# One PSUM bank set aside for the first upper products of each expert's first chunk

## The chip, the cores and the metric

The kernel runs on one core of one Trainium2 chip. The metric is the device time of one execution in microseconds (us). Three runs of the kernel before gave 606.06, 604.7 and 606.04 us, median 606.04.

## What is computed

The reference chains three parts. First comes attention (2 batches, 8 heads, 768 positions, head size 64; each position sees 4 sink positions and a window of 128). Its output, 1536 tokens of 512 numbers, goes through a dense pair of products (512 to 2048 to 512, with a leaky step between). Last comes a layer of 8 experts, and the change lies there:

```
logits = x @ w_gate;  expert_idx = argmax(logits)
# each token takes the next free row of its expert, up to capacity = 384
h = max(einsum('ecd,edf->ecf', disp, w1), 0)     # 512 -> 1024, "upper"
y = einsum('ecf,efd->ecd', h, w2)                # 1024 -> 512, "lower"
out[i] = gate_w[i] * y[expert_idx[i], pos[i]]
```

With the reference's inputs the router sends 715, 147, 16, 240, 4, 20, 277 and 117 tokens to experts 0 to 7.

## The kernel before, in words

An expert's rows are cut into chunks of 128: a capacity of 384 gives up to three chunks per expert, written (e, 0), (e, 1), (e, 2). The number of rows of an expert is known only while the kernel runs. So chunk (e, 0) is always computed, and chunks (e, 1) and (e, 2) stand in conditional parts, one inside the other (`further_chunks`, `guard`, branches on line L1327). Chunk (0, 0) is computed earlier in most cases; the experts' stage only repeats it under a condition on `more` (L1366 and L1367). With these inputs the `more` part is skipped, (0, 1), (0, 2), (1, 1), (3, 1), (6, 1) and (6, 2) are computed, and the conditional parts of experts 2, 4, 5 and 7 are skipped whole.

One chunk is computed in four steps. `turn_in` (L431 to L433) turns the rows with four TensorE transposes and splits them into a high and a low half (ACT, then DVE). `expert_up` (L1262, L1267) makes two products of 512 columns, 12 matmuls each (three per slice of 128, for the two halves of both factors); ACT evicts each from PSUM through a Relu into `hh`. `turn_hidden` (L1282 to L1286) turns the hidden rows, ACT (`hth`) and DVE (`htl`) split them. `expert_down` (L1298) adds up 24 matmuls, a scaled eviction `yo` follows (L1305, or L1303 in the last chunk), and POOL scatters the rows to the output (L1308). The weights arrive by DMA in pieces (L1214 on the SP queue) and are split by ACT (L1196) and DVE (L1197).

The stage has all eight PSUM banks. They are named es0 to es2, et0 to et3 and eo0, and the list `every` has them in that order. Three rings share them: "t" (es0 to es2) for what is turned, "u" (et0, et1, et2) for upper products, "y" (et3, eo0) for lower products. `next_bank` goes round a ring at build time, whether a conditional part will run or not:

```python
banks = {"t": every[:3], "u": every[3:6], "y": every[6:]}
```

In this ring an expert's three chunks take six upper banks, so (e, 0) always gets et0 and et1, (e, 1) et2 and et0, (e, 2) et1 and et2. Expert 0 is the exception in the text of the program: `more` holds (0, 0) with et0 and et1, and (0, 1) follows with et2 and et0.

The order on each engine is the order of the program's text. What one engine waits for on another is a count of that other's finished instructions. A skipped conditional part is left through an instruction of its own on each engine (an event semaphore on the branch's line): it waits until the engine's own earlier work is done and then adds to the count all that the skipped part would have added. So a matmul that writes a bank last read by ACT in a skipped conditional part waits until ACT itself has come past that part.

Around the end of the dense part stand these steps, in TensorE's order: `first_y` (L489, lower product of chunk (0, 0), in bank eo0, evicted by ACT at L496), the skipped `more` part (L1366, L1367), `turn_in_slot(1, 0)` (L431, into the bank that `next_bank("y")` gives), and `further_chunks(0, 1)` (L1249, L1327, L1262). From expert 1 on, the loop does `expert_up(e, 0)`, two turns in, `expert_down(e - 1, 0)`, `turn_hidden(e, 0)` and then the conditional part of e; the next thing on TensorE after that part is `expert_up(e + 1, 0)`.

Of the kernel before, what the change touches and what calls it, by code (L numbers as in the profile page):

```python
# [35 lines left out]
def attention_mlp_moe_kernel(  # L36
# [84 lines left out]
    def slot(tag, dt=F32R):  # L121
        slot_n[tag] = slot_n.get(tag, 0) + 1
        return slot_pool[tag].tile([P, SW], dt, tag=tag, name=f"{tag}_{slot_n[tag]}", bufs=1)
# [7 lines left out]
    for bl in range(NT // XB):  # L131
        for kp in range(KD // 2):
            for hl in range(2):
                t = slot(f"x{(bl * (KD // 2) + kp) * 2 + hl}")
# [182 lines left out]
    def bank(tag, name, shape=(P, 512)):  # L317

        if not shared:
            tag = tag[-1].replace("x", "t")  # L320
            return psum[0].tile(list(shape), F32, tag=tag, name=name, bufs=n_bank[tag])
        banks_ = bank_sets[tag[:-1]][tag[-1]]
        n = bank_at[tag] = bank_at.get(tag, -1) + 1
        return psum[0].tile(
            list(shape), F32, tag=f"b{banks_[n % len(banks_)]}", name=name, bufs=1
        )
# [295 lines left out]
    with ExitStack() as actx:  # L622
# [12 lines left out]
        for n in range(QA):  # L635
            t = ap_c.tile([P, 2, S], F32, name=f"qa{n}")
# [36 lines left out]
        if small:  # L673
            for n in range(3):
                t = ap_c.tile([P, 2, 4, D1], F32, name=f"vsk{n}")
                nc.gpsimd.memset(t, 0.0)
                vsks.append(t)
                t = ap_c.tile([P, P], F32, name=f"pk{n}")
# [190 lines left out]
        for b in range(B):  # L869
            for hp in range(H // 2):  # L870
# [3 lines left out]
                for i0 in range(0, NQ, 2):  # L874
                    t = Item()
                    t.st, t.n, t.nm, t.units = st, len(groups), f"{st.nm}_{i0}", []
                    for ii in range(min(2, NQ - i0)):
                        u = Item()
# [32 lines left out]
        def at(xs, n):  # L911
            return xs[n] if 0 <= n < len(xs) else None
# [23 lines left out]
        for n in range(nu + 11):  # L936
            u = at(units, n)
# [292 lines left out]

    ep.append(ctx.enter_context(tc.tile_pool(name="ep", bufs=2, side="right")))
    every = [bank(tag, f"e{tag}{n}") for tag in "sto" for n in range(n_bank[tag])]
    banks = {"t": every[:3], "u": every[3:6], "y": every[6:]}
    bank_n = {}

    def next_bank(nm):
        n = bank_n[nm] = bank_n.get(nm, -1) + 1
        return banks[nm][n % len(banks[nm])]
# [15 lines left out]
    def expert_up(e, c):  # L1254
        ups = experts[e][0]
        x = tx.pop((e, c))
        h = ep[0].tile([P, F], F32, tag="hh", name=f"hh{e}_{c}", bufs=1)
        for o in range(0, F, 512):
            ph = next_bank("u")
            for kk in range(KD):  # L1260
                for n, (xl, wl) in enumerate(((0, 0), (0, 1), (1, 0))):
                    nc.tensor.matmul(  # L1262
                        ph, x[xl][:, kk * P:(kk + 1) * P],
                        ups[kk][wl][:, o:o + 512],
                        start=(kk == 0 and n == 0), stop=(kk == KD - 1 and n == 2),
                    )
            nc.scalar.activation(h[:, o:o + 512], ph, AF.Relu)  # L1267
        hid[e, c] = h
# [44 lines left out]
    def further_chunks(e, c):  # L1313

        if c == NCH:
            return
        if NCH > 3:
            for c in range(1, NCH):
                with guard(e, c):
                    if c > 1:  # L1320
                        fetch(e, c)
                        turn_in(e, c)
                    expert_up(e, c)
                    turn_hidden(e, c)
                    expert_down(e, c)
            return
        with guard(e, c):  # L1327
            expert_up(e, c)
            turn_hidden(e, c, (lambda: turn_in(e, c + 1)) if c + 1 < NCH else None)
            expert_down(e, c)  # L1330
            further_chunks(e, c + 1)
# [7 lines left out]
    for e in range(E):  # L1339

        splits_to((e + 1) * PER - (e == 1))
        if e:
            expert_up(e, 0)
# [96 lines left out]
```

## Time and profile before

| what | value |
|---|---|
| runs, us | 606.06, 604.7, 606.04 (median 606.04) |
| profiled execution, its own time | 605.23 us |
| its span, first to last instruction | 603.4 us |
| granted TensorE clock, mean over the span | 0.996 |
| TensorE (PE) busy with matmuls | 580.9 us, 96% |
| VectorE (DVE), ScalarE (ACT), GpSimd (POOL) busy | 419.8, 346.6, 83.8 us |

The execution's own time is 1.8 us longer than its span; what lies around the span is not broken down. The experts' stage runs from about 420 us to the end. A busy share is a mean over stages; what a change in one place is worth is read from the waits in that place.

### The profile page before, as it was taken

How to read it: one execution, taken by the hardware profiler on the slowest of the kernel's cores; microseconds unless marked ns; L12 is line 12 of the kernel's file. 1: busy time of each engine (PE TensorE's matmuls, PEld its weight loads, DVE VectorE, ACT ScalarE, POOL GpSimd, SP SyncE). 2: the span in 40 equal slices, each digit the busy share in tenths (PEclk: the TensorE clock that was granted, in tenths of full speed). 3: DMA queues.
4: the chain of work that ended last, by engine and by line, in shares of the span. 5: the costliest groups of instructions: out<-in, count | busy, mean ns of one | idle time of the engine just before them, and what ended most of it. 6: DMA issues, size and time to landing. Idle time of an engine off the chain costs nothing. (4 is left out here: it accounts for less than half of the span.)

```text
span 603.4 us, 9071 instructions
## 1 busy us (share of the span) xinstructions
PE 580.9 (96%) x3174; PEld 485.2 (80%) x3174; DVE 419.8 (70%) x872; ACT 346.6 (57%) x641; POOL 83.8 (14%) x128
## 2 busy tenths in 40 slices
PE   7999999999989999999999999999999999999994
PEld 6999998878767888888899898976777777778783
DVE  6578878689999568974577787965326783885240
ACT  5677776566565545444466677854238474775330
POOL 5011433210000000000200021113210211111011
PEclk9999999999999999999999999999999999999998
DMA  7969742224641660000100022334918692993000
GB/s 226 329 209 307 209 142 71 71 70 145 200 146 68 216 272 2 0 1 0 54 19 2 0 78 74 113 110 136 348 45 295 216 380 102 348 356 127 18 21 35
DMA packets 32996, 83.86 MB, mean 139 GB/s; under 512 B 3646, under 2 KB 4206, under 8 KB 32944
## 3 DMA queue, kind: packets, MB, share of 16 engines
q1 hardware_dynamic: 28800, 71.66, 35.6%
q0 software_dynamic: 4144, 11.53, 5.5%
q8 instruction: 30, 0.49, 0.3%
q14 instruction: 22, 0.18, 0.1%
HBM read 68.75 MB, written 16.31 MB: 141 GB/s over the span
## 5 line engine op out<-in xcount | busy, mean ns | idle before, releaser
L362 PE MATMUL h<-x,r 128*128 128x512 f32 (+1 forms) x768 | 148.6, 340 | 3.2 <-DVE r L274 3.1
L362 PEld LDWEIGHTS h<-x,r 128*128 128x128 f32 x768 | 120.5, 189 | 22.8 <-DVE r L274 5.2
L393 PE MATMUL acc<-r,gh 128*128 128x512 f32 x384 | 120.5, 395 | 0.0
L393 PEld LDWEIGHTS acc<-r,gh 128*128 128x128 f32 x384 | 69.9, 188 | 14.2
L393 PE MATMUL acc<-r,gl 128*128 128x512 f32 x192 | 75.9, 395 | 0.0
L736 PE MATMUL s<-ka,qa 128*128 128x260 f32 x192 | 59.9, 399 | 4.2 <-DMA qa<-in_q_dram 3.9
L846 PEld LDWEIGHTS o<-vr,pT 128*128 128x128 f32 x352 | 55.5, 192 | 4.8
L375 DVE SCALAR_TENSOR_TENSOR g<-gn,nalpha,g 128x512 f32<-128x512 f32 (+1 forms) x64 | 39.4, 615 | 24.3 <-ACT g L374 24.2
L274 DVE TENSOR_TENSOR r<-wo,r 128x1024 fp32r<-128x1024 f32 x31 | 37.9, 1224 | 24.7 <-ACT r L271 24.5
L373 ACT ACTIVATE gn<-h 128x512 f32<-128x512 f32 (+1 forms) x64 | 31.4, 491 | 40.8 <-PE h L362 40.3
L846 PE MATMUL o<-vr,pT 128*128 128x65 f32 x352 | 53.6, 251 | 0.0
L1267 ACT ACTIVATE hh<-et 128x512 f32<-128x512 f32 x26 | 15.6, 599 | 65.5 <-PE et L1262 59.2
L1153 POOL DMA_INDIRECT xs<-x,slot_i x12 | 14.4, 1198 | 264.3 <-ACT g L374 164.4
L382 ACT CAST gh<-g 128x512 fp32r<-128x512 f32 (+1 forms) x64 | 32.9, 514 | 28.1 <-DVE g L375 27.9
L755 ACT ACTIVATE p<-sx,mn 128x260 f32<-128x260 f32 (+1 forms) x96 | 42.9, 488 | 9.4 <-DVE mn L751 8.9
L271 ACT CAST r<-wo 128x1024 fp32r<-128x1024 f32 (+1 forms) x33 | 33.8, 1025 | 22.6 <-PE acc L393 21.7
L768 PE MATMUL pt<-ident,p 128*128 128x128 f32 x176 | 46.5, 279 | 0.0
L751 DVE CUSTOM_DVE_ANT_0 sx<-s,mask 128x260 f32<-128x260 f32 (+1 forms) x96 | 36.9, 400 | 13.7 <-PE s L736 9.7
L393 PEld LDWEIGHTS acc<-r,gl 128*128 128x128 f32 x192 | 36.1, 188 | 8.6
L274 DVE TENSOR_TENSOR r<-wi,r 128x1024 fp32r<-128x1024 f32 x30 | 36.7, 1222 | 2.3 <-ACT r L271 2.3
L385 DVE TENSOR_TENSOR gl<-g,gh 128x512 fp32r<-128x512 f32 (+1 forms) x64 | 35.4, 553 | 1.6 <-ACT gh L382 1.6
L736 PEld LDWEIGHTS s<-ka,qa 128*128 128x128 f32 x192 | 30.9, 200 | 5.2 <-issue 3.8
(204 smaller groups left out, 1101.5 us busy)
## 6 DMA issues: line engine op xcount, KB each, us to landing
raw_all<-in_w_dram SPq DMA_DIRECT2D x36, 512.0 KB, 5.7
more_raw<-in_w_dram SPq DMA_DIRECT2D x28, 512.0 KB, 6.3
raw_all<-in_w_in_dram SPq DMA_DIRECT2D x8, 1024.0 KB, 6.3
raw_all<-in_w_out_dram SPq DMA_DIRECT2D x8, 1024.0 KB, 5.0
xs<-r SPq DMA_DIRECT2D x8, 771.0 KB, 10.1
rows<-xs POOLq DMA_DIRECT2D x20, 256.0 KB, 5.8
vr<-in_v_dram SPq DMA_DIRECT2D x4, 780.0 KB, 5.0
out_dram<-fill SPq DMA_DIRECT2D x2, 1536.0 KB, 13.2
```

The source lines that it names most:

```text
L271: nc.scalar.copy(hi[:, x], w[:, x])
L274: eng.tensor_sub(lo[:, x], w[:, x], hi.bitcast(F32)[:, x])
L362: nc.tensor.matmul(ph[:, :TB], wi[wl][:, kk, f0:f0 + P], xT_at(kk, tok, TB, xl), start=(n == 0), stop=(n == 3 * KD - 1),)
L375: nc.vector.scalar_tensor_tensor(out=g, in0=gn, scalar=nalpha[:, f:f + 1], in1=g, op0=ALU.mult, op1=ALU.add)
L382: nc.scalar.copy(gh, g)
L385: nc.vector.tensor_sub(gl, g, gh.bitcast(F32))
L393: nc.tensor.matmul(acc[t], g[a][:, t * P:(t + 1) * P], wo[w][:, f % FG, :], start=(f == 0 and x == 0), stop=(f == KF - 1 and x == 2),)
L736: nc.tensor.matmul(s[:, o:o + w], st.qa[:, h, toks], st.ka[:, c:c + w], start=True, stop=True, skip_group_check=True,)
L751: nc.vector.tensor_tensor_reduce(out=x[:, :w], in0=u.s[h][:, :w], in1=m[:, :w], scale=-scale, scalar=BIG, op0=ALU.add, op1=ALU.min, accum_ ...
L755: nc.scalar.activation(t.p[:, u.ii, h, :w], x[:, :w], AF.Exp, bias=t.mn[:, c:c + 1], scale=-1.0)
L768: nc.tensor.transpose(pt[:, c * P:(c + 1) * P], t.p[:, u.ii, h, u.offs[n]:u.offs[n] + P], ident,)
L846: nc.tensor.matmul(t.o[:, 2 * u.ii + h, :], u.pT[:, w], vr[:, hv * NQ + j, :], start=(not sg and n == 0), stop=(n == len(js) - 1), skip_gr ...
```

## The change

The ring "u" shrinks to et0 and et1. A new ring "v" has et2 and et1, in that order. The upper products of first chunks of experts 1 to 7 take "u", all others (chunks (e, 1) and (e, 2), and everything of expert 0) take "v". So et0 holds nothing but the first upper product of a first chunk from expert 1 on. The two banks of the ring "y" are exchanged.

```diff
-    banks = {"t": every[:3], "u": every[3:6], "y": every[6:]}
+
+    banks = {
+        "t": every[:3], "u": every[3:5], "v": [every[5], every[4]], "y": [every[7], every[6]],
+    }
@@ expert_up
-            ph = next_bank("u")
+            ph = next_bank("v" if c > 0 or e == 0 else "u")
```

No instruction is added or removed on any engine; line numbers behind the change grow by three. What differs is the bank that a product is written to, and with it what its first matmul waits for.

TensorE from the end of the skipped `more` part on, before: four transposes of `turn_in_slot(1, 0)`, the guard, and the first upper product of chunk (0, 1). In the names, `r0` holds the rows, `r1` the turned rows of (0, 1), `x0` to `x3` the weights.

```order
L1367 UNCONDITIONAL_BRANCH [waits PE_49]
L431 MATMUL eo0_4698<-ident_66,r0_17_4596 128x128 [waits DMASW6_49,Activation_49]
L431 MATMUL eo0_4698<-ident_66,r0_17_4596 128x128 x3
L1249 TENSOR_LOAD cnt_i_117
L1249 ISA x2
L1327 COMPARE_AND_BRANCH
L1262 MATMUL et2_4696<-x0_3_3830,r1_17_4668 128x512
L1262 MATMUL et2_4696<-x1_3_3831,r1_17_4668 128x512
L1262 MATMUL et2_4696<-x0_3_3830,r1_17_4668 128x512 [waits DVE_49]
```

The same place now:

```order
L1370 UNCONDITIONAL_BRANCH [waits PE_49]
L431 MATMUL et3_4697<-ident_66,r0_17_4596 128x128 [waits DMASW6_49,PE_49]
L431 MATMUL et3_4697<-ident_66,r0_17_4596 128x128 x3
L1252 TENSOR_LOAD cnt_i_117
L1252 ISA x2
L1330 COMPARE_AND_BRANCH
L1265 MATMUL et2_4696<-x0_3_3830,r1_17_4668 128x512 [waits Activation_49]
L1265 MATMUL et2_4696<-x1_3_3831,r1_17_4668 128x512
L1265 MATMUL et2_4696<-x0_3_3830,r1_17_4668 128x512 [waits DVE_49]
```

The transposes moved from eo0 to et3 and lost their wait on ACT. The first matmul of chunk (0, 1) still writes et2, but now waits on ACT, where it waited on nothing before: et2 is now the bank in which the skipped `more` part has its own first upper product.

TensorE behind the conditional part of expert 2, before: the first upper product of chunk (3, 0). `wi4` to `wi6` are high halves of its weights (ACT), `wo4` and `wo5` low halves (DVE).

```order
L1327 UNCONDITIONAL_BRANCH [waits PE_49] x2
L1262 MATMUL et0_4694<-wi4_3_5310,xh3_0_5290 128x512 [waits Activation_49]
L1262 MATMUL et0_4694<-wo4_3_5311,xh3_0_5290 128x512 [waits DVE_49]
L1262 MATMUL et0_4694<-wi4_3_5310,xl3_0_5291 128x512
L1262 MATMUL et0_4694<-wi5_3_5314,xh3_0_5290 128x512
L1262 MATMUL et0_4694<-wo5_3_5315,xh3_0_5290 128x512 [waits DVE_49]
L1262 MATMUL et0_4694<-wi5_3_5314,xl3_0_5291 128x512
L1262 MATMUL et0_4694<-wi6_3_5318,xh3_0_5290 128x512
```

The same place now:

```order
L1330 UNCONDITIONAL_BRANCH [waits PE_49] x2
L1265 MATMUL et0_4694<-wi4_3_5310,xh3_0_5290 128x512 [waits Activation_49]
L1265 MATMUL et0_4694<-wo4_3_5311,xh3_0_5290 128x512 [waits DVE_49]
L1265 MATMUL et0_4694<-wi4_3_5310,xl3_0_5291 128x512
L1265 MATMUL et0_4694<-wi5_3_5314,xh3_0_5290 128x512 [waits Activation_49]
L1265 MATMUL et0_4694<-wo5_3_5315,xh3_0_5290 128x512 [waits DVE_49]
L1265 MATMUL et0_4694<-wi5_3_5314,xl3_0_5291 128x512
L1265 MATMUL et0_4694<-wi6_3_5318,xh3_0_5290 128x512 [waits Activation_49]
```

The order is the same. Before, one wait of the first matmul covered all later ones on ACT, since it was for an eviction that comes after the weights' splits in ACT's order, inside the conditional part. Now each slice of weights has a wait of its own, so the first wait is only for the split of `wi4`.

## Rows read from the trace of the kernel before

**Rows 1.** The page: span, granted clock in 40 slices, one row of DMA issues.

```profile
span 603.4 us, 9071 instructions
...
PEclk9999999999999999999999999999999999999998
...
raw_all<-in_w_dram SPq DMA_DIRECT2D x36, 512.0 KB, 5.7
```

**Rows 2.** Waits of PE, whole span: who for whom, us in total, times, longest.

```profile
PE h L362 <- DVE r L274: 3.1, 4, 0.9
PE et L1262 <- ACTq L1327: 2.3, 3, 0.8
...
PE et L1262 <- PEq L1327: 0.8, 2, 0.4
PE eo L431 <- ACT x L496: 0.8, 1, 0.8
```

**Rows 3.** Timeline of PE, 419.8 to 422: start, us taken, instruction, [idle before <- releaser].

```profile
419.82 0.40 PE L489 MATMUL first_y<-wi,x 128*128 128x512 f32 x1
421.00 0.66 PE L431 MATMUL eo<-ident,r 128*128 128x128 f32 x4 [0.78 <-ACT x L496]
421.83 0.49 PE L1262 MATMUL et<-x,r 128*128 128x512 f32 x1 [0.18 <-issue]
```

**Rows 4.** Line L1367 (skipped part): ns min/median/max, first and last start.

```profile
L1367 PEldq EVENT_SEMAPHORE  x1: 51/51/51, 420.3 to 420.3; - x1
...
L1367 ACTq EVENT_SEMAPHORE  x1: 17/17/17, 424.1 to 424.1; - x1
```

**Rows 5.** Timeline of ACT, 420.2 to 425.6.

```profile
420.26 0.69 ACT L496 ACTIVATE x<-first_y,first 128x512 f32<-128x512 f32 x1
423.01 1.05 ACT L1196 CAST x<-raw_all 128x1024 fp32r<-128x1024 f32 x1 [2.06 <-DMA raw_all<-in_w_dram]
424.21 0.59 ACT L432 CAST r<-eo 128x512 fp32r<-128x512 f32 x1 [0.16 <-ACTq L1367]
```

**Rows 6.** Timeline of PE, 481.8 to 484, around the skipped part of expert 2.

```profile
481.89 1.03 PE L1282 MATMUL es<-ident,hh 128*128 128x128 f32 x8
483.70 0.50 PE L1262 MATMUL et<-wi,xh 128*128 128x512 f32 x1 [0.77 <-ACTq L1327]
```

**Rows 7.** Line L1327, 482 to 484: both engines' way out of that part.

```profile
L1327 PEldq EVENT_SEMAPHORE  x1: 51/51/51, 483.0 to 483.0; - x1
...
L1327 ACTq EVENT_SEMAPHORE  x1: 17/17/17, 483.6 to 483.6; - x1
```

**Rows 8.** Timeline of ACT, 478 to 484.

```profile
478.00 2.96 ACT L1196 CAST wi<-more_raw 128x1024 fp32r<-128x1024 f32 x3
482.52 1.07 ACT L1285 CAST hth<-es 128x512 fp32r<-128x512 f32 x2 [1.57 <-PE es L1282]
483.71 1.05 ACT L1196 CAST x<-more_raw 128x1024 fp32r<-128x1024 f32 x1
```

**Rows 9.** Timelines of DVE, then ACT, 470 to 562: splits and evictions near that part.

```profile
479.29 3.49 DVE L1197 TENSOR_TENSOR wo<-more_raw,wi 128x1024 fp32r<-128x1024 f32 x3
...
489.61 0.60 ACT L1267 ACTIVATE hh<-et 128x512 f32<-128x512 f32 x1 [1.52 <-PE et L1262]
```

**Rows 10.** Timeline of PE, 468.8 to 470, behind a skipped inner part.

```profile
468.87 0.40 PE L1298 MATMUL et<-r,htl 128*128 128x512 f32 x1
469.68 0.50 PE L1262 MATMUL et<-x,xh 128*128 128x512 f32 x1 [0.42 <-PEq L1327]
```

**Rows 11.** Line L1327, 469.2 to 469.7: that way out on PE.

```profile
L1327 PEldq EVENT_SEMAPHORE  x1: 51/51/51, 469.3 to 469.3; - x1
...
L1327 PEldq COMPARE_BRANCH  x1: 169/169/169, 469.5 to 469.5; - x1
```

**Rows 12.** Timeline of PE, its last matmul.

```profile
595.25 0.40 PE L1298 MATMUL et<-r,htl 128*128 128x512 f32 x1
```

**Rows 13.** Stretches: us, busy PE, PEld, DVE, ACT, POOL, then PEclk, DMA share, GB/s.

```profile
595.70:598.50 2.80, 0.00 (x0) 0.00 (x0) 0.00 (x0) 0.67 (x1) 0.97 (x1) 1.00 0.12 45
598.60:603.40 4.80, 0.00 (x0) 0.00 (x0) 0.00 (x0) 0.00 (x0) 0.00 (x0) 0.50 0.04 14
```

**Rows 14.** Timeline of PE, 3 to 9: its first matmuls.

```profile
3.87 3.81 PE L736 MATMUL s<-ka,qa 128*128 128x260 f32 x8 [3.87 <-DMA qa<-in_q_dram]
...
7.89 1.11 PE L736 MATMUL s<-ka,qa 128*128 128x260 f32 x4
```

## The prediction

> **What bounds the kernel now.** I read the page first. The span is 603.4 us and the granted clock is full in nearly all slices [rows 1]; TensorE is busy 96% of the span, so a time that TensorE loses or gains is lost or gained at the end, unless a later wait takes it up. The second view is TensorE's list of waits [rows 2]. In the experts' stage three entries bear on this change: 2.3 us in three waits on ACT's branch queue before an upper product (0.77 each), 0.8 us in two waits on TensorE's own branch queue, and one wait of 0.8 us of the transposes into eo on ACT's eviction L496. The third view is the timeline at those places.
>
> The three waits of 0.77 are the exits from the skipped parts of experts 2, 4 and 5. In the first, the last transposes end at 481.89 + 1.03 = 482.92 and the next upper product starts at 483.70 [rows 6]. TensorE's own way out is at 483.0, ACT's at 483.6 [rows 7], because ACT still has two copies to do that those transposes feed, until 482.52 + 1.07 = 483.59 [rows 8]. So TensorE waits for a skipped part, of which it needs nothing, until ACT has walked past it.
>
> The same pair of exits stands at the skipped `more` part at 420, and much wider: TensorE is out at 420.3, ACT at 424.1 [rows 4]. ACT is late because its split at 423.01 waited 2.06 us for a weight transfer and took 1.05 [rows 5]. Before the change nobody pays for it: the upper product of chunk (0, 1) starts at 421.83 [rows 3], since et2 is not touched by the skipped part.
>
> **The change, part by part.** No instruction and no transfer is added, and no queue changes its order; only waits change.
>
> *Transposes of `turn_in_slot(1, 0)`, eo0 to et3.* They no longer wait for L496, which ends at 420.26 + 0.69 = 420.95 [rows 5]. They can follow TensorE's own exit at 420.3 [rows 4] and start some 0.2 to 0.4 later, so at 420.5 to 420.7 in place of 421.00 [rows 3]. Alone this would be worth 0.3 to 0.5. I count nothing, since the next step waits for something later.
>
> *First upper product of (0, 1): a new wait on ACT.* The text gives everything of expert 0 the ring "v", so the skipped `more` part and chunk (0, 1) now share et2, and the order shows the new wait. It ends when ACT is out of the `more` part, at 424.1 [rows 4]. After such an exit TensorE starts together with ACT's next instruction: 483.70 against ACT's 483.71 [rows 6, 8]. ACT's next instruction behind `more` is at 424.21 [rows 5], so TensorE starts at 424.20 and not 421.83: **+2.37 us**. What queues behind it is the whole experts' stage on TensorE. ACT and DVE follow TensorE there and do not catch the time up: I find no wait of TensorE behind this place that ends on a transfer [rows 2]. The bounds are what ACT's exit depends on: a transfer that lands 0.3 earlier or later moves it by as much.
>
> *Three exits (experts 2, 4, 5): the wait on ACT goes.* et0 is now read by no conditional part. The first matmul waits for its weights' split only; ACT's splits ended at 478.00 + 2.96 = 480.96 [rows 8], DVE's at 479.29 + 3.49 = 482.78 [rows 9], both before TensorE's exit at 483.0. What is late next is that exit. How soon TensorE starts after it, the trace does not show for this kind of exit. The nearest row is a skipped inner part: exit 469.3, a branch of 0.17, product at 469.68 [rows 10, 11], so 0.38 with the branch and 0.21 without; the whole part has no such branch at its end. The upper product then starts between 483.1 (the 0.1 from ACT's exit to its next instruction [rows 7, 8]) and 483.38, and gains between 0.6 and 0.32. I take 0.21 after 483.0, a gain of 0.49, three times: **-1.47 us**, bounds -0.96 and -1.8. Behind it the cover holds: ACT sits idle 1.52 us before it evicts the second upper product [rows 9], so it can be reached 0.5 sooner, and the hidden rows are needed only after two turns in and a lower product. By the Trainium skill, Advanced Engine Details and Errata, section Control Flow Timing, an unconditional branch takes about 51 ns; the trace has 169 here. An estimate with the page's price would leave 0.33 after the exit and a gain of 1.1 in all.
>
> *Exits after a computed chunk (1, 1) and (3, 1).* They wait for TensorE's own queue, 0.42 each [rows 2, 10]; the change does not touch that. The second upper product (et1) waits for ACT too, but 12 matmuls later, when ACT is long out. Nothing.
>
> *The lower products in exchanged banks.* They meet the same partners as before with the two names swapped. Nothing.
>
> So the waits alone give 2.37 - 1.47 = **+0.90 us**, between +0.3 and +1.7.
>
> *The clock.* The new wait leaves TensorE almost idle: its last product ends at 419.82 + 0.40 = 420.22 [rows 3], four transposes take 0.66 from about 420.6, and then nothing comes until 424.20, some 2.9 us. No idle time inside the kernel before was longer than 0.9 once it had begun to multiply [rows 2], and the clock stayed full. At the end the last matmul ends at 595.65 [rows 12]; the granted clock is 1.00 until 598.5 and 0.50 (1.2 of 2.4 GHz) from 598.6 on [rows 13]: it fell 2.9 us after the last work. The new wait is as long as the only idle stretch that is known to have ended at the lower level, and three times the longest that is known to be harmless. I take it that the clock falls in most executions. The price of one slow stretch: the first eight matmuls took 3.81 us (0.48 each), four of the same kind later 1.11 (0.28 each) [rows 14]; eight at the later pace are 2.2, so the stretch cost 1.6. It can be less where the slow stretch begins within the wait: bounds 0 and 2.0. I take **+1.5 us**. The Trainium skill, TensorE: Matmul & The Clock Gate, section HAM oscillation, tells of a kernel in which each wait for a transfer between bursts of matmuls put the clock back to half; by that rule the burst behind this wait runs slow, which would be this term.
>
> **Sum.** 605.23 (the profiled execution's own time) + 2.37 - 1.47 + 1.5 = 607.63. That execution lies 0.81 under the median of the three runs, between them (604.7 to 606.06). The mean of the four is 605.51, so I add 0.28: **607.9 us**, 0.4% above 605.5 and 0.3% above the median. A measurement of this kernel can tell about 0.3%, 1.8 us, from no change.
>
> **The rivals.**
>
> *The new wait comes, but the clock stays.* 2.9 us of idle time is at the edge of what the rows bear out, with four transposes just ahead of it, and a stretch known to be slow lies only at the program's two ends. Then the time is 605.51 + 0.90 = 606.4, within 0.3%.
>
> *The new wait is short, and the gain is left: not slower.* The wait's length hangs on one transfer, for which ACT's split waited 2.06 us [rows 5]. Each us that it lands sooner takes one us from the loss; at 0.9 sooner, exit at 423.2, loss and gain are even; at 2.0 sooner ACT leaves at 422.1, the wait costs 0.3, and the sum is -1.2: 604.3. If chunk (0, 1) did not wait at all, the gain of the earlier transposes would come on top, -1.9: 603.6. Against it: nothing ahead of that transfer is changed, and its kind takes 5.7 us at the median [rows 1].
>
> *The exits give nothing.* Another wait (a split of weights, a slow restart of TensorE behind its own exit) could take the place of ACT's exit. Then +2.37 stands alone, 607.9 at full clock and 609.4 with the slow stretch. Against it: the splits end before the exit, as worked out above.
>
> **How the numbers follow.** Forecast (new wait, slow stretch) 0.46; clock stays 0.36; short wait 0.08; exits give nothing 0.10. The range takes in the forecast and the first rival with their bounds, from 605.5 (+0.3, a little under) to 609.2 (+1.7 and the full 2.0). The forecast lies hardly above what can be told from no change, so a sixth of it counts as "same": slower 0.38 + 0.10 and a little of the first rival, 0.49; same 0.08 + 0.33 + 0.05, 0.46; faster only from a short wait, 0.05.
>
> **What would show it right or wrong.** In the changed kernel's waits, the three entries of 0.77 on ACT's branch queue should be gone, with upper products starting some 0.2 after TensorE's exits; one new entry of about 2.9 should stand at the first upper product of chunk (0, 1), released by ACT's queue on the `more` branch; and the wait of 0.8 on L496 should be gone. The granted clock in the stretches from 424 to 428 tells the forecast from its first rival: 1.00 throughout, and the forecast is wrong by 1.5. If chunk (0, 1) starts at 422 or sooner, the main term is wrong.

## The result and the profile after

The changed kernel takes 608.75 us (median of 6 runs, 608.29 to 609.24), the kernel before beside it 605.54 (6 runs, 604.7 to 606.52). The ratio is 1.0053, 95% interval 1.004 to 1.0066: slower by 3.2 us. The forecast was 607.9.

The page of the changed kernel's profiled execution (608.65 us) answers to [rows 1]; the last row is the granted clock in 40 slices:

```profile
span 606.9 us, 9070 instructions
...
PEclk9999999999999999999999999999899999999998
```

The clock, full in all inner slices before, has an 8 in the slice from 425 to 440 us.

TensorE's waits, to be read against [rows 2] (who for whom, us in total, times, longest):

```profile
PE et L1265 <- ACTq L1370: 3.6, 1, 3.6
PE h L362 <- DVE r L274: 3.1, 4, 0.9
PE et L1265 <- PEq L1330: 1.1, 4, 0.4
```

The three waits of 0.77 on ACT's branch queue are gone, and so is the one on L496. One wait of 3.6 stands in their place, on ACT's way out of the skipped `more` part (now L1370). Its place in the timeline of PE answers to [rows 3]:

```profile
420.34 0.40 PE L489 MATMUL first_y<-wi,x 128*128 128x512 f32 x1
421.14 0.63 PE L431 MATMUL et<-ident,r 128*128 128x128 f32 x4 [0.40 <-PEq L1370]
425.40 7.19 PE L1265 MATMUL et<-x,r 128*128 128x512 f32 x24 [3.64 <-ACTq L1370]
432.43 0.60 PE L1285 MATMUL es<-ident,hh 128*128 128x128 f32 x4
```

The transposes no longer wait for ACT, and then the first upper product of chunk (0, 1) does, for 3.64 us. The line's own view shows the exit that it waits for, later than in [rows 4]:

```profile
L1370 PEldq EVENT_SEMAPHORE  x1: 51/51/51, 420.8 to 420.8; - x1
...
L1370 ACTq EVENT_SEMAPHORE  x1: 17/17/17, 425.3 to 425.3; - x1
...
L1370 DVEq EVENT_SEMAPHORE  x1: 21/21/21, 426.6 to 426.6; - x1
```

The wait is for ACT alone, which reads et2 in the skipped part: the product starts at 425.40, before DVE is out. ACT's timeline there, against [rows 5], shows why it is late:

```profile
420.77 0.69 ACT L496 ACTIVATE x<-first_y,first 128x512 f32<-128x512 f32 x1
424.26 1.04 ACT L1196 CAST x<-raw_all 128x1024 fp32r<-128x1024 f32 x1 [2.80 <-DMA raw_all<-in_w_dram]
```

ACT waits 2.80 us for a weight transfer, splits it, and only then walks past the branch. The stretches behind, with the columns of [rows 13]:

```profile
421.80:425.00 3.20, 0.00 (x0) 0.00 (x0) 0.00 (x0) 0.74 (x1) 2.44 (x2) 1.00 0.93 326
425.10:428.40 3.30, 3.00 (x7) 2.42 (x8) 1.92 (x2) 0.79 (x2) 0.00 (x0) 0.50 1.06 396
428.50:432.00 3.50, 3.50 (x17) 2.83 (x16) 0.00 (x0) 0.60 (x1) 0.00 (x0) 1.00 1.03 245
```

TensorE had no work for 3.2 us, and at about 425 its granted clock went to 0.50, 1.2 of 2.4 GHz. Until 428.4 it began 7 matmuls; in the next stretch, of about the same length, 17.

At the exit from expert 2's skipped part, the place of [rows 6], the gain stands:

```profile
486.93 1.03 PE L1285 MATMUL es<-ident,hh 128*128 128x128 f32 x8
488.12 0.47 PE L1265 MATMUL et<-wi,xh 128*128 128x512 f32 x1 [0.15 <-PEq L1330]
```

And the two exits there, as in [rows 7]:

```profile
L1330 PEldq EVENT_SEMAPHORE  x1: 51/51/51, 488.0 to 488.0; - x1
...
L1330 ACTq EVENT_SEMAPHORE  x1: 17/17/17, 488.7 to 488.7; - x1
```

TensorE starts 0.1 after its own exit and 0.6 before ACT's.

Start times cut the difference into pieces:

| from, to (start times of matmuls on PE) | before, us | after, us | difference |
|---|---|---|---|
| span's start, last `first_y` | 419.82 | 420.34 | +0.52 |
| last `first_y`, first product of (0, 1) | 2.01 | 5.06 | +3.05 |
| that product, first turn of the hidden rows | 5.57 | 7.03 | +1.46 |
| that turn, last matmul (595.25, 598.30) | 167.85 | 165.87 | -1.98 |
| last matmul, end of the span | 8.15 | 8.6 | +0.45 |

Two of these starts stand in no row above, the turn in the kernel before (427.40, against 432.43 after) and the last matmul of the changed kernel:

```profile
427.40 0.60 PE L1282 MATMUL es<-ident,hh 128*128 128x128 f32 x4
```

```profile
598.30 0.40 PE L1301 MATMUL eo<-r,htl 128*128 128x512 f32 x1
```

The first and the last piece are work that the change does not touch, and differ between executions. The three in the middle make +2.53 us.

### The profile page after: what moved, and what is told of

It reads as the page before. It is cut to its first block, busy times and chain, and to the rows that moved or that the text cites. A ratio compares the mean times of both kernels' runs of the same rounds, so it can differ in the third digit from the quotient of the medians.

```text
span 606.9 us, 9070 instructions
## 1 busy us (share of the span) xinstructions
PE 582.5 (96%) x3174; PEld 486.6 (80%) x3174; DVE 419.6 (69%) x872; ACT 346.6 (57%) x641; POOL 84.2 (14%) x128
## 5 line engine op out<-in xcount | busy, mean ns | idle before, releaser
L1289 DVE TENSOR_TENSOR htl<-es,hth 128x512 fp32r<-128x512 f32 x26 | 17.2, 683 | 29.1 <-ACT hth L1288 29.1
```

## The experiments

The theory: chunk (0, 1) waits for ACT to leave the skipped `more` part, since the two now share et2; the clock falls during that wait; and each of three exits gives 0.6 us back. All eight kernels ran beside the kernel before (605.05 to 606.93 us in the first four, median 606.21; 604.77 to 607.57, median 606.06, in the others).

**The repeated first chunk of expert 0 back in ring u**

```diff
-            ph = next_bank("v" if c > 0 or e == 0 else "u")
+            ph = next_bank("v" if c > 0 else "u")
```

> Only the repeated first chunk of expert 0 goes back to the ring u (et0, et1), all else as in the changed kernel, so chunk (0, 1) shares et2 with no skipped part. Theory (the loss is the wait of chunk (0, 1) for ACT's way out of the skipped part, plus a slow stretch of the clock behind it; each of the three exits gains 0.62): no wait on that branch, clock 1.00 from 420 to 600, three exits with a product 0.11 after TensorE's own exit; 605.5 - 1.9 - 0.3 = 603.3 us, ratio 0.996. Rival (the loss comes from the exchanged banks of lower products or from the smaller ring u): about 608.7, as the changed kernel.

Measured: 603.59 us, ratio 0.9965 (0.9952 to 0.9978). Waits and timeline of PE:

```profile
PE et L1265 <- PEq L1330: 0.8, 2, 0.4
...
PE et L1265 <- ACTq L1370: 0.2, 1, 0.2
...
420.91 2.99 PE L1265 MATMUL et<-x,r 128*128 128x512 f32 x12 [0.23 <-issue]
424.09 3.02 PE L1265 MATMUL et<-x,r 128*128 128x512 f32 x12 [0.19 <-ACTq L1370]
```

One condition in the choice of the bank takes the change from slower to faster. The expectation missed a detail: a wait on that branch is left, 0.19, at the second product of (0, 1), since et1 is still shared.

**Expert 0's sharing alone**

```diff
-    banks = {"t": every[:3], "u": every[3:6], "y": every[6:]}
+    banks = {"t": every[:3], "u": every[3:6], "v": [every[5], every[4]], "y": every[6:]}
...
-            ph = next_bank("u")
+            ph = next_bank("v" if e == 0 else "u")
```

> The kernel before, with expert 0 alone on et2 and et1; experts 1 to 7 and the lower products as before. Theory: the same wait of 3 to 3.6 us at chunk (0, 1) and the same slow stretch, while the three exits keep their 0.77: 608.7 + 1.9 = 610.6 us, ratio 1.008. Rival (the exits gave nothing at the end of the program, for something later takes it up): 608.7.

Measured: 610.32 us, ratio 1.0072 (1.0058 to 1.0086). Waits, timeline and a stretch of PE:

```profile
PE et L1262 <- ACTq L1367: 2.7, 1, 2.7
PE et L1262 <- ACTq L1327: 2.3, 3, 0.8
...
425.73 8.21 PE L1262 MATMUL et<-x,r 128*128 128x512 f32 x24 [2.71 <-ACTq L1367]
433.77 0.60 PE L1282 MATMUL es<-ident,hh 128*128 128x128 f32 x4
...
424.30:431.00 6.70, 5.27 (x12) 4.13 (x13) 1.92 (x2) 1.63 (x2) 0.80 (x1) 0.50 1.06 314
```

This part alone makes the loss, and the three exits, left as they were, still stand in the list with 2.3 us. By the ratios the kernel is 1.2 us slower than the changed one, less than the three exits give elsewhere (1.9); the two intervals overlap, and the wait and the slow stretch are not the same here, so this run does not price the exits. The wait is 2.71 and not the expected 3 to 3.6, and the low clock lasted 6.7 us, twice as long as in the changed kernel.

**The wait filled with products**

```diff
             turn_in_slot(1, 0, "r4", next_bank("y"))
+            w = experts[0][0][0][0]
+            for n in range(12):
+                nc.tensor.matmul(every[3], w[:, :P], w[:, :512], start=(n == 0), stop=(n == 11))
```

The added products are not part of what is computed; nothing reads them.

> The changed kernel with 12 more products of 512 columns into et0 in front of chunk (0, 1), 2.8 us of TensorE work that waits for nothing new and whose result is not used. Theory with the clock: the wait ends at the same ACT exit, TensorE is busy during it, the granted clock stays 1.00, and chunk (0, 1) takes 5.6 us as before: 608.7 - 1.4 = 607.3 us. Rival (the whole loss is the wait, the clock costs nothing): 608.7; and if the added products delay anything, more.

Measured: 607.97 us (11 runs, 606.63 to 609.25), ratio 1.0026 (1.0015 to 1.0037). Timeline and stretches:

```profile
422.57 3.01 PE L1378 MATMUL et<-x 128*128 128x512 f32 x12
426.84 5.78 PE L1265 MATMUL et<-x,r 128*128 128x512 f32 x24 [1.26 <-ACTq L1370]
432.46 0.60 PE L1285 MATMUL es<-ident,hh 128*128 128x128 f32 x4
...
425.60:426.80 1.20, 0.00 (x0) 0.00 (x0) 0.02 (x1) 1.04 (x1) 0.00 (x0) 1.00 0.99 321
426.90:432.40 5.50, 5.50 (x24) 4.50 (x25) 1.79 (x2) 1.16 (x2) 0.00 (x0) 1.00 1.04 305
```

With 3.0 us more work in it the wait ends as before at ACT's exit (426.8 in this execution), the clock stays at 1.00 and chunk (0, 1) takes 432.46 - 426.84 = 5.62 us and not 7.03. This separates the two losses: the wait costs its length whether TensorE works in it or not, and the slow stretch costs 1.4 more. In the medians the ratio falls from 1.0053 to 1.0026, 0.27% or 1.6 us; the intervals of the two ratios do not overlap. The profiled execution is the slowest of the eleven: from the turn on it took 1.05 us more than the changed kernel's (166.92 against 165.87), 0.55 of it in a wait for a split of weights, so the gain is read from the medians and not from its length.

**The split behind the skipped part**

```diff
-        splits_to((e + 1) * PER + PW1 + 1 * (e == 0) - (e == 1))
+        splits_to((e + 1) * PER + PW1 - (e == 1))
```

> The changed kernel with one split of expert 1's lower weights moved from before the skipped part to behind it, so that ACT does not wait for that transfer ahead of the branch; the banks are those of the changed kernel. Theory: ACT leaves the skipped part about 1 us after its eviction of the first lower product, near 422; chunk (0, 1) starts at about 422, the clock stays 1.00: 605.5 - 1.9 + 0.2 = 603.8 us. Rival (the wait hangs on something else, the transfer only happens to end there): about 608.7.

Measured: 603.32 us, ratio 0.9953 (0.9939 to 0.9968). The line of the branch and PE's timeline:

```profile
L1370 ACTq EVENT_SEMAPHORE  x1: 17/17/17, 421.0 to 421.0; - x1
...
421.42 5.71 PE L1265 MATMUL et<-x,r 128*128 128x512 f32 x24 [0.22 <-issue]
```

The banks are shared as in the changed kernel, and the wait on them is gone, since ACT leaves at 421.0, without waiting for a transfer ahead of the branch. So the length of the wait is that of the transfer and its split.

**The exchange of the lower banks alone**

```diff
-    banks = {"t": every[:3], "u": every[3:6], "y": every[6:]}
+    banks = {"t": every[:3], "u": every[3:6], "y": [every[7], every[6]]}
```

> The kernel before with the two banks of lower products exchanged, nothing else. Theory: the transposes behind the skipped part no longer wait for the eviction of the first lower product and start 0.3 after TensorE's own exit, so chunk (0, 1) starts 0.4 sooner against the last of the first lower products; the three exits keep 0.77; 606.2 - 0.4 = 605.8 us, within 0.3%. Rival (the exchange costs something, or is worth the whole of the difference between the repaired kernel and the exits): 604.3 or 607.

Measured: 606.33 us, ratio 0.9999 (0.9988 to 1.0011). PE's timeline:

```profile
421.26 0.63 PE L431 MATMUL et<-ident,r 128*128 128x128 f32 x4 [0.30 <-PEq L1367]
422.11 2.99 PE L1262 MATMUL et<-x,r 128*128 128x512 f32 x12 [0.23 <-issue]
426.15 3.02 PE L1262 MATMUL et<-x,r 128*128 128x512 f32 x12 [1.04 <-ACTq L1367]
```

The transposes start sooner after TensorE's exit, as expected, but the second product of (0, 1), in et0, waits 1.04 for the same exit of ACT. In the kernel before it did not, though it always depended on it: there ACT's exit came while TensorE still worked on the first product. In this execution ACT's exit came 5.5 us after the last `first_y` began, later than in any other profile here, so how often the gain is lost that way is not shown. The exchange alone gives nothing that can be told; the expected 0.4 us would be a ratio of 0.9993, which the interval holds too.

**The exits alone**

```diff
-    banks = {"t": every[:3], "u": every[3:6], "y": every[6:]}
+    banks = {"t": every[:3], "u": every[3:5], "v": [every[5], every[4]], "y": every[6:]}
...
-            ph = next_bank("u")
+            ph = next_bank("v" if c > 0 else "u")
```

> The kernel before with ring u cut to et0 and et1 for all first chunks, expert 0's too, and ring v (et2, et1) for chunks 1 and 2; lower products as before. Theory: the three exits give 0.62 each, nothing else changes: 606.2 - 1.9 = 604.3 us, ratio 0.997. Rival (the gain of the repaired kernel came from the exchange): 605.8 or above.

Measured: 604.06 us, ratio 0.9969 (0.9957 to 0.9981), 0.3% or 1.9 us faster. In its waits no entry on ACT's branch queue is left:

```profile
PE et L1262 <- PEq L1327: 0.8, 2, 0.4
PE eo L431 <- ACT x L496: 0.8, 1, 0.8
```

**Both repairs**: the edit of the first experiment and that of the fourth.

> Both repairs in one: the repeated first chunk of expert 0 in ring u, and the split of expert 1's lower weights behind the skipped part. Theory: each removes the same wait, so together they give what the later split gave alone, 603.3 us, and neither product of chunk (0, 1) waits for ACT. Rival (two separate losses): about 602, lower than either.

Measured: 603.93 us, ratio 0.9961 (0.9944 to 0.9978), with neither product waiting for ACT:

```profile
422.45 5.71 PE L1265 MATMUL et<-x,r 128*128 128x512 f32 x24 [0.33 <-issue]
```

No gain on top of either, so both remove the same loss. The four kernels with the exits' gain and without the wait (0.9953, 0.9961, 0.9965, 0.9969) cannot be told apart by their intervals; each beats the kernel before and the changed one.

**The kernel before with the later split**: the edit of the fourth experiment on the kernel before.

> The kernel before with the split of expert 1's lower weights moved behind the skipped part, banks as before. Theory: in the kernel before nothing on TensorE waits for ACT's way out of the skipped part, so the move is worth nothing: 606.2 us, within 0.2%. Rival (the later split is a gain by itself, and the repaired kernel's time is no evidence on the wait): about 604.

Measured: 605.75 us, ratio 0.9992 (0.9983 to 1.0001). The later split is worth nothing that can be told by itself. In the changed kernel it is worth 1.0053 against 0.9953.

## Why the prediction was right, point by point

*What bounds.* Right: TensorE's starts carry every piece of the table through to its last matmul.

*Transposes, counted at nothing.* Right: they lost their wait and start 0.3 to 0.4 after TensorE's exit. In the one profile of the exchange alone the gain is given back one product later, even without the new wait.

*The new wait, +2.37.* The mechanism was right: the place, the releaser, and the start together with ACT's next instruction (425.40 against 425.43). The size was too small: 3.05, and 3.64 for the entry in the list that was put at about 2.9. The term rested on one execution, in which ACT's exit came at 424.1, 4.3 us after the last `first_y` began (419.82, [rows 3, 4]). In the other profiles with the split ahead of the branch that distance was 5.0 (after: 425.3 less 420.34) and, in the order of the experiments, 4.7, 4.5, 5.3, 5.5 and 4.5. What sets the landing of that transfer was not followed; the execution that the forecast was made from was the quickest of the seven. The bounds of 0.3 either way were too narrow.

*Three exits, -1.47.* Right in kind, and each a little larger: 0.62, since TensorE starts 0.1 after its own exit [rows 7 against the exits above] and not 0.21. Three times 0.62 is 1.86, a little past the term's bound of 1.8. The piece of the table in which they lie gives -1.98, and the exits alone moved the median by 1.9 to 2.0.

*The clock, +1.5.* The mechanism was right, and so was the size: 7.03 - 5.57 = 1.46 in the changed kernel, nothing in the filled wait. The size was worked out from the program's first eight matmuls [rows 14], as a stretch at the lower level. The view of that stretch in the kernel before prints a clock of 1.00:

```profile
3.80:8.00 4.20, 4.13 (x11) 3.23 (x12) 1.87 (x8) 1.31 (x3) 3.75 (x17) 1.00 0.82 264
```

The first clock record of that trace begins only at 8.0 us, so the level at which those eight ran is not shown. Their pace speaks for the lower one (0.48 each, and 0.28 for the four of the same kind from 7.89 on), but that step was argued. What the runs show of the price: 3.00 us of TensorE's work at 0.50 cost 1.46, and with expert 0's sharing alone 5.27 us of work cost 2.47, about half of the time worked at that level.

That the clock falls in most executions can be read from the mean granted clock, which is on record for each timed execution. It is 0.992 to 0.995 in the six of the changed kernel (mean 0.994), 0.994 to 0.998 in the 46 of the kernel before beside the experiments (mean 0.996) and 0.995 to 0.997 in the eleven of the filled wait. A stretch of 3.3 us at 0.50 lowers the mean by 3.3 * 0.5 / 606.9 = 0.0027. For the two executions at 0.995 it cannot be told singly.

*The sum.* The forecast's terms gave +2.4, the three pieces of the profile +2.53, because a wait 0.7 too small and gains 0.5 too small nearly cancel, which is luck. The measured +3.2 (2.4 to 4.0 by the interval) holds both.

*The rivals.* That the clock stays fell with the trace and the mean clocks. That the wait would be short fell too, though its mechanism is real: the later split is that rival, made by hand, and it ends where it was put, on the faster side. That the exits give nothing fell with the exits alone.

## What to carry to other kernels

Here a bank that was shared with a conditional part cost a wait until the engine that reads the bank there (ACT) had walked past that part, even though the part was skipped; an engine that left later (DVE) was not waited for. So before banks are dealt out anew, list for each skipped part what the engines that use the shared bank in it have queued ahead of its branch, above all a wait for a transfer. A buffer that removes such a wait in three places can add a longer one in a fourth, and the special case (here expert 0, whose first chunk stands in a condition) is the one to follow through the order. The two waits left empty here, of 3.64 and 2.71 us, had to be priced twice: with their own length, and with a slow burst behind them.

## What the runs showed of the hardware that was not expected

TensorE started 0.1 us after its own way out of a whole skipped part, against 0.38 behind a skipped inner part [rows 10, 11], where a branch of 0.17 follows and the rest is time between the instructions.

The price of a fall of the clock was not the same twice. In the changed kernel TensorE idled for 3.64 us, the clock went to 0.50 some 0.3 before the end of that time, and 3.3 us at that level made a loss of 1.46. With expert 0's sharing alone it idled for 0.78, did four transposes and idled for 2.71; the clock went to 0.50 at about 424.3, 1.4 before the end of that time, for 6.7 us, and chunk (0, 1) took 433.77 - 425.73 = 8.04 us, a loss of 2.47. An idle time of 1.26 behind the filled part of the wait left the clock at 1.00. Why the low level lasted twice as long in one of them stays open.
